# Second MLP's first product in pairs of tiles by Strassen's seven quarter products, in a fused attention and two-MLP kernel

## The chip, the core and the metric

The kernel runs on one core of a Trainium2 chip. The metric is the device time of one launch in microseconds (us). Engines are named TensorE (PE in the profile, its weight loads PEld), VectorE (DVE), ScalarE (ACT), GpSimd (POOL) and SyncE (SP, which issues all transfers here).

## What is computed

A linear attention with 4 batches, 8 heads, 576 positions and head size 64 gives 2304 rows of 512 values. Two MLPs follow, and it is the second that matters here:

```python
def _moe_ref(x, w_in, w_out):            # 2304 x 512, 512 x 2048, 2048 x 512
    h = x @ w_in
    g = np.maximum(0.01 * h, h)
    return (g @ w_out).astype(np.float32)

def _moe2_ref(x, w_in, w_out, g_ln):     # 2304 x 512, 512 x 1024, 1024 x 512
    h = x @ w_in
    h_max = np.max(h, axis=-1, keepdims=True)
    e = np.exp(h - h_max)
    sm = e / (np.sum(e, axis=-1, keepdims=True) + 1e-09)
    solu = h * sm
    mu = np.mean(solu, axis=-1, keepdims=True)
    var = np.mean((solu - mu) ** 2, axis=-1, keepdims=True)
    ln = (solu - mu) / np.sqrt(var + 1e-06) * g_ln
    return (ln @ w_out).astype(np.float32)
```

## The kernel before

**Tiles.** The 2304 rows are 18 tiles of 128, and for MLP 1 nine blocks j of two tiles. Large products run in float16 with each operand split into a high and a low half, and three of the four half products are taken: (high, high), (high, low), (low, high). So the first product of MLP 2 for one tile (`mlp2_in`) is 3 x 4 x 2 = 24 matmuls of 512 columns, into a PSUM tile `h2` of two banks, and the second product (`mlp2_out`) is 3 x 8 = 24 more into one bank of `h1`. MLP 1's first product is `st1` (tile `h1`, eight steps p for a block, L1090), its second `st2` (tile `y`, L1134).

**Order.** No engine's order is written out by hand. Every step is a generator that asks a planner (class `Issue`) for an engine with an expected duration and a priority; the planner runs a clock of its own, gives each free engine the waiting step with the lowest number, and emits instructions in that order. On the chip every engine then works through its queue in that order and waits by semaphores. `get` and `put` take and give back room (a PSUM bank, a buffer), `wait` and `set` are events. The numbers here: `st2` 1000, `st1` 1001.5, `mlp2_out` 1002, `mlp2_in` 1003 for tiles 0 to 12 and 1001 for the last five (`X["tail"]`). MLP 2 begins when its weights have been split ("mlp2").

**One tile of MLP 2 before.** After the 24 matmuls `mlp2_mid` takes the row maximum on VectorE (L1274), the exponential on ScalarE (L1279), the product with e (L1286, PSUM read again, after which `h2` is free), statistics (L1291), a power on GpSimd (L1294), the normalization (L1299), the high half on GpSimd (L1304) and the low half on VectorE (L1306), then two transposes through the DMA queue (L1311) into `lnT`, of which there are two. `mlp2_out` (L1324) multiplies, ScalarE copies the result out (L1333), SyncE stores it (L1339). Weights: `w1` and `w2` hold those of MLP 1, `W["i"]` (wi) and `W["o"]` (wo) those of MLP 2. `XY[j]` holds the transposed halves of block j's rows, first as input of MLP 1, later as input of MLP 2. `y_cut` makes the latter; `u` is the factor that undoes the scalings.

Of the kernel before, what the change touches and what calls it, by code (L numbers as in the profile page):

```python
# [23 lines left out]

X = {'NF': 1, 'bufs': {'qe': 3, 'v': 1, 'qf': 2, 'ke': 3, 'hl': 1, 'x': 2, 'g': 9, 'sg': 1, 'qT': 2, 'x16': 2, 'scr': 2, 'T': 1, 'wraw': 4, 'raw': 1, 'y16': 3, 'lnT': 2, 'l16': 2, 'kf': 4, 'v16': 3}, 't0': 38.107, 'tb': 187.479, 'w1': 54.105, 'w1s': -59.238, 'w2': 352.332, 'w2s': 14.253, 'b0': -113.048, 'b1': -6.038, 'dk': 42.281, 'dq': 74.634, 'dl': 206.254, 'c1': -41.937, 'c2': -59.523, 'pw2': 104.035, 'wlo': [1, 3, 8, 11, 13, 14, 16, 17, 25, 28, 31, 34, 36, 37, 38, 39], 'vd': 105.739, 'warm': 300, 'psq': ['k0', 'q0', 'q3', 'k6', 'q6', 'q7', 'q8', 'q9'], 'ep': ['k1', 'k12', 'k14', 'k16', 'k3', 'k4', 'k5', 'k6', 'k7', 'q0', 'q1'], 'te': ['k00', 'k01', 'k11', 'k40', 'k41', 'x10', 'x11'], 'KH': [2, 3], 'vb': 118.863, 'ya': [0, 1, 4, 6, 7, 9, 11, 12, 13, 14, 15, 16, 17, 18, 19, 20, 22, 23, 24, 27, 29, 31], 'EK': [0, 1, 2, 3, 6, 7, 8], 'pkv': 56.661, 'tail': 5, 'off': {'q1': -150.9, 'w15': 261.17, 'w4': 14.2, 'w23': -532.04, 'w18': 143.18, 'w24': -228.68, 'w28': 52.21, 'q10': 208.4, 'k8': -54.41, 'q5': 362.46, 'w7': 254.87, 'w25': 296.88, 'w12': 299.75, 'w9': -116.63, 'w19': 106.43, 'w31': 120.17, 'w27': -435.77, 'k11': -354.41, 'q16': -125.64, 'w5': 228.93, 'k9': -15.0, 'q2': 245.68, 'w8': 98.43, 'w14': -147.85, 'w30': -294.84, 'e1': 30.87, 'w26': 198.68, 'k13': 18.32, 'q0': 10.8, 'k0': -175.63, 'k7': 93.8, 'q13': 199.99, 'k2': -2.3, 'k16': -339.39, 'w22': -96.81, 'k6': -286.1, 'k4': 122.7, 'q8': 12.64, 'v0': -2.93, 'w20': -418.66, 'w16': 175.2, 'w0': 352.98, 'q6': 324.81, 'v2': 1.52, 'w17': -233.24, 'w13': 60.91, 'w3': -282.06, 'v1': 51.23, 'e2': 80.0, 'w1': 21.19, 'k15': -13.38, 'q3': -61.35, 'w2': -459.82, 'q7': 171.44, 'q4': 93.37, 'w11': 210.27, 'q12': -65.87, 'k5': 105.62, 'q15': 86.28, 'w10': 85.38, 'k14': -4.24, 'w29': -114.4, 'q17': -227.35, 'k12': -171.67, 'v3': 295.13, 'w21': -21.91, 'q11': -31.65, 'q9': 12.76, 'k17': 83.15, 'q14': 50.45, 'k1': 72.93, 'e3': 132.73, 'w6': -32.87, 'k3': -224.59, 'k10': 456.53}, 'pe': -535.604}

# [154 lines left out]
def linear_attention_moe_kernel(  # L181
# [92 lines left out]
    def t1(nm, n=1):  # L274
        return tiny.tile([128, n], F32, name=nm, tag=nm, bufs=12 if nm in ("sq", "sc", "s") else 8)

# [20 lines left out]
    def chain(c):  # L297
        return (True,) if c else ()
# [886 lines left out]
    def mlp2_weights():  # L1185
# [16 lines left out]
        stage.close()  # L1202
        P2["e"] = ctx.enter_context(tc.tile_pool(name="e2", bufs=2, side="right"))
        yield "set", "mlp2"

    def mlp2_weight(nm, src, sp, wp, gl):
# [15 lines left out]
        def fin(r):  # L1222
            yield from scale_of_max(r, inv, s)
            if nm == "i":
# [14 lines left out]
    def mlp2_in(a, z):  # L1239
        yield "wait", "mlp2"  # L1240
        for i in range(a, z):
# [4 lines left out]
            for j, (a, w) in enumerate(((0, 0), (0, 1), (KC, 0))):  # L1246
# [5 lines left out]
                yield "op", "PE", 1.71, mm, *chain(j < 2)  # L1252
            yield "go", mlp2_mid(i, ps.rearrange("p a f -> p (a f)")), i
        if z < NTILE:
            yield "go", mlp2_in(z, NTILE), 1001

# [12 lines left out]
    def mlp2_mid(i, ps):  # L1269
# [45 lines left out]
    def mlp2_out():  # L1315
        for i in range(NTILE):
# [51 lines left out]
    with tc.manual_schedule():  # L1368
# [57 lines left out]
```

## Time and profile before

| | |
|---|---|
| Median of 3 runs | 709.07 us (708.9 to 710.46) |
| Span of the profiled execution, first to last instruction | 707.2 us |
| TensorE busy / VectorE busy | 692.8 / 481.4 us |
| ScalarE busy / GpSimd busy | 361.5 / 132.8 us |
| Mean granted clock of TensorE | 0.998 of full speed |

How to read it: the profile is one execution; the runs are timed apart from it, over the whole launch, so the median stands somewhat above the span. [...] In the chain that ended last each step is followed back to what released it. In the last quarter of the span the kernel runs nothing but MLP 2.

### The profile page before, as it was taken

The numbers are of one execution on the slowest core, as the hardware profiler recorded it, in microseconds if no ns is written. First come the engines' busy times: TensorE is split into PE (matmuls) and PEld (weight loads), VectorE is DVE, ScalarE is ACT, GpSimd is POOL, SyncE is SP. The second block draws the span as 40 slices with busy tenths as digits, with TensorE's granted clock in tenths as the row PEclk, the third lists the DMA queues.
The fourth block names the chain that finished last, engine by engine and source line by source line (L and its number), as shares of the span: only waits on it lengthen the run. The fifth ranks groups of instructions, "written<-read, shape, count | busy, mean of one in ns | idle before, by whom it ended". The sixth has DMA issues, their size and how long they took to land.

```text
span 707.2 us, 13423 instructions
## 1 busy us (share of the span) xinstructions
PE 692.8 (98%) x5162; PEld 457.2 (65%) x5162; DVE 481.4 (68%) x1191; ACT 361.5 (51%) x770; POOL 132.8 (19%) x177
## 2 busy tenths in 40 slices
PE   7989999999999999999999999999999999999997
PEld 7889885587775667767676767676654444444443
DVE  6878888798765666756856478842267757757870
ACT  4768987797766664666745437463232122111211
POOL 2010220432311110011201022632001101101220
PEclk9999999999999999999999999999999999999999
DMA  9886986694735433722745667101013442432254
GB/s 289 239 255 195 251 237 142 123 180 112 148 72 94 96 71 84 120 67 52 130 76 89 126 216 192 66 1 30 1 31 75 104 75 54 102 69 60 59 103 106
DMA packets 183599, 81.22 MB, mean 115 GB/s; under 512 B 146416, under 2 KB 175088, under 8 KB 183536
## 3 DMA queue, kind: packets, MB, share of 16 engines
q1 hardware_dynamic: 183536, 80.37, 49.0%
q8 instruction: 40, 0.66, 0.4%
q14 instruction: 23, 0.19, 0.1%
HBM read 41.75 MB, written 4.72 MB: 66 GB/s over the span
## 4 chain that ended last, share of the span: by engine, by line
PE 75%; issue 7%; DMA 6%; ACT 5%; DVE 4%; POOL 1%; SPq 0%; POOLq 0%; ACTq 0%; DVEq 0%
PE h L1090 17%; PE y L1134 16%; PE h L1324 13%; PE h L1250 13%; DMA v<-in_v_dram 4%; PE h L1084 4%; PE kv L850 3%; ACT qe L786 2%; PE y L1130 1%; PE a L1008 1%; DVE mx L771 1%; PE a L763 1%; PE a L764 1%; DMA qT<-qf 1%; ACT ke L786 1%
## 5 line engine op out<-in xcount | busy, mean ns | idle before, releaser
L1134 PE MATMUL y<-w,g 128*128 128x512 f16 x768 | 176.0, 379 | 0.0
L1090 PEld LDWEIGHTS <-w 128*128 128x128 f16 x1536 | 148.2, 98 | 25.1 <-issue 1.1
L1134 PEld LDWEIGHTS <-g 128*128 128x128 f16 x768 | 73.9, 98 | 77.3 <-DVE g L1108 0.7
L1090 PE MATMUL h<-xy,w 128*128 128x256 f16 x960 | 111.8, 273 | 0.0
L1324 PE MATMUL h<-wo,lnT 128*128 128x512 f16 x432 | 96.0, 379 | 0.0
L1108 DVE TENSOR_TENSOR g<-h,g 128x512 f16<-128x512 f32 x64 | 44.0, 687 | 54.7 <-ACT g L1107 54.5
L1324 PEld LDWEIGHTS <-lnT 128*128 128x128 f16 x432 | 42.3, 98 | 51.0
L1250 PE MATMUL h<-wi,xy 128*128 128x512 f16 x336 | 75.1, 379 | 0.0
L1106 ACT ACTIVATE h<-h 128x512 f32<-128x512 f32 x64 | 38.1, 595 | 71.3 <-PE h L1090 70.9
L1090 PE MATMUL h<-xT,w 128*128 128x256 f16 x576 | 67.8, 273 | 0.1
L1279 ACT ACTIVATE e<-h,nb,u 128x1024 f32<-128x1024 f32 x18 | 21.7, 1203 | 76.5 <-DVE nb L1276 76.5
L1250 PEld LDWEIGHTS <-xy 128*128 128x128 f16 x336 | 32.9, 98 | 38.6
L786 ACT ACTIVATE qe<-a,nb,sc 128x128 f32<-128x128 f32 x128 | 47.1, 468 | 15.2 <-DVE nb L777 13.8
L771 DVE TENSOR_REDUCE mx<-a 128x4 f32<-128x512 f32 x63 | 41.4, 683 | 9.8 <-PE a L764 7.3
L1333 ACT ACTIVATE osb<-h,c_out 128x512 f32<-128x512 f32 x18 | 12.3, 686 | 64.4 <-PE h L1324 42.1
L873 POOL TENSOR_SCALAR qf<-qe 128x512 f16<-128x512 f32 x32 | 20.3, 634 | 110.4 <-ACT qe L786 84.5
L1107 ACT ACTIVATE g<-h 128x512 f16<-128x512 f32 x64 | 38.7, 604 | 1.2
L1294 POOL TENSOR_TENSOR rs<-ve,mhalf 128x1 f32<-128x1 f32 x18 | 9.9, 549 | 151.7 <-DVE ve L1293 151.7
L876 DVE SCALAR_TENSOR_TENSOR qf<-qe,qf 128x512 f16<-128x512 f32 x32 | 23.6, 738 | 16.0 <-POOL qf L873 16.0
L786 ACT ACTIVATE ke<-a,nb,sc 128x128 f32<-128x128 f32 x64 | 23.3, 468 | 16.8 <-DVE nb L777 15.0
L672 POOL TENSOR_TENSOR scr<-raw 128x1024 f32<-128x1024 f32 (+1 forms) x8 | 14.4, 1801 | 91.1 <-DMA raw<-in_q_dram 80.8
L1274 DVE TENSOR_REDUCE mx<-h 128x1 f32<-128x1024 f32 x18 | 21.9, 1216 | 12.1 <-PE h L1250 12.1
(197 smaller groups left out, 1146.0 us busy)
## 6 DMA issues: line engine op xcount, KB each, us to landing
wraw<-in_moe_w_in_dram SPq DMA_DIRECT2D x24, 512.0 KB, 5.7
wraw<-in_moe_w_out_dram SPq DMA_DIRECT2D x24, 512.0 KB, 4.7
v<-in_v_dram SPq DMA_DIRECT2D x12, 512.0 KB, 4.4
raw<-in_k_dram SPq DMA_DIRECT2D x8, 512.0 KB, 4.2
raw<-in_q_dram SPq DMA_DIRECT2D x8, 512.0 KB, 4.7
out_dram<-osb SPq DMA_DIRECT2D x16, 256.0 KB, 2.4
v<-in_v_dram SPq DMA_DIRECT2D x6, 128.0 KB, 3.7
lnT<-l SPq DMA_TRANSPOSE x36, 3.2
```

Source lines behind the costliest of these rows:

```text
L771: yield "op", "V", 0.6, lambda: V.tensor_reduce(out=u["mx"][:, hh::2], in_=w["ps"], axis=AX.X, op=ALU.max)
L786: A.activation(out=x[:, h, :], in_=w["ps"][:, h, :], func=AF.Exp, scale=st["sc"], bias=u["nb"][:, 2 * h + hh:2 * h + hh + 1])
L876: yield "op", "V" if stay else "V2", 0.62, lambda: V.scalar_tensor_tensor(out=w["f"][:, :, 1, :], in0=w["e"], scalar=2.0 ** 14, in1=w["f"] ...
L1084: PE.matmul(ps[:, f, :], lhsT=stash(w1, c * KC + kc)[:, o:o + 128], rhs=xT[j][:, kc, :], start=(kc == 0), stop=(kc == KC - 1))
L1090: PE.matmul(ps[:, f, :], lhsT=w1[:, c * KC + kc, w, o:o + 128], rhs=xT[j][:, :, xo + kc, :], start=(n == 0), stop=(n == 3 * KC - 1))
L1106: yield "op", "A", 0.48, lambda: A.activation(out=ps, in_=ps, func=AF.Prelu, scale=2.0 ** -19, alpha=0.01)
L1107: yield "op", "A", 0.48, lambda: A.activation(out=gg[:, 0], in_=ps, func=AF.Copy)
L1108: yield "op", "V", 0.6, lambda: V.tensor_tensor(out=gg[:, 1], in0=ps, in1=gg[:, 0], op=ALU.subtract)
L1134: PE.matmul(y_ps[j][t], lhsT=gg[:, a, f, ts], rhs=w2[:, 2 * p + f, w, :], start=(ends[0] and f == 0 and n == 0), stop=(ends[1] and f == 1 ...
L1250: PE.matmul(ps[:, f, :], lhsT=yT[i][:, a + c, :], rhs=W["i"][:, 2 * c + f, w, :], start=(j == 0 and c == 0), stop=(j == 2 and c == KC - 1))
L1274: yield "op", "V", 1.13, lambda: V.tensor_reduce(out=mx, in_=ps, axis=AX.X, op=ALU.max)
L1324: PE.matmul(ps, lhsT=t[:, a, f, :], rhs=W["o"][:, f, w, :], start=(j == 0 and f == 0), stop=(j == 2 and f == KF2 - 1))
```

## The change

Tiles 0 to 3 go as before. From tile 4 on two tiles j are taken together (`mlp2_pairs`). The pair's input is cut in quarters (tile, half of the 512 inputs), the weights in quarters (half of the inputs, half of the 1024 outputs), and the four result quarters come from seven quarter products instead of eight (Strassen's scheme in Winograd's form). One quarter product is 3 x 2 = 6 matmuls of 512 columns. Five of the seven take a sum of input quarters, of weight quarters, or both:

- `weight_sums` makes four sums of weight quarters (`T_`), for two input chunks c: high and low halves are added to float32, quarters subtracted, and the sums split in halves again (`sum_cut`). The first set adds on VectorE, the second on GpSimd (`X["wv"]`). They go into the place of `w1`, when `st1` of the last block has used it.
- `x_sums` makes four sums of input quarters (`S_`) for each pair, also in the place of `w1`; one float32 buffer (`S32`), three split ones (`S16`).
- In `mlp2_pairs` one PSUM half `pa` is written three times, each time on top of the former, and ScalarE copies it out after each (`seen`). VectorE adds such a copy to the other products and in the same instruction takes the row maximum (`joined`, a `tensor_tensor_reduce`). The results, `h`, lie in SBUF in six buffers (`H`): four in the place of `w2`, two in that of `XY[0]` and `XY[1]`.
- `pair_mid` and `pair_ln` do what `mlp2_mid` did: exponentials, the product with e fused with the sum for the mean, squares on ScalarE for the variance, scaling on ScalarE, halves, transposes. `lnT` gets four more buffers in the place of `w2`.
- Some scalings are one or two powers of two smaller. The table X loses `tail: 5` and gets `first: 2` (two blocks as before), `nh: 4`, `ws: 500`, `wv: [4, 0]`. Priorities: pairs 1001, their seventh product 1000.5, sums of weights 500, sums of inputs j - 1.

```diff
         if z < NTILE:
-            yield "go", mlp2_in(z, NTILE), 1001
+            yield "go", mlp2_pairs(z // 2, NB), 1001
...
+    def sums_open():
+
+        yield "wait", "w2i"
+        for c in range(2):
+            yield "go", weight_sums(c), X["ws"] + c
+        for p in range(6, 8):
+            yield "wait", ("s1", NB - 1, p)
+        yield "put", "S32"
...
+            for n in (8, 10, 14):
+                free_s.append(region(w1, n, 2).rearrange("p (a t k m) -> p a t k m", a=2, t=2, m=128))
+                yield "put", "S16"
...
+        for n in range(8):
+            yield "wait", ("s2", NB - 1, n)
+            if n < X["nh"]:
+                free_h.append(region(w2, 2 * n, 2).bitcast(F32))
+                yield "put", "H"
+            else:
+                free_t.append(region(w2, 2 * n, 2).rearrange("p (a f m) -> p a f m", a=2, m=128))
+                yield "put", "lnT"
...
+    def weight_sums(c):
+
+        b0, t0 = (0, 4) if c == 0 else (8, 0)
+        for p in range(4) if c == 0 else range(4, 6):
+            yield "wait", ("s1", NB - 1, p)
+        if c:
+            yield "wait", ("T", 0)
+        x = [region(w1, b0 + b, 1).bitcast(F32) for b in range(4)]
...
+        def whole(b, n):
+            if b < X["wv"][c]:
+                return "op", "V2", 0.69, lambda: V.tensor_tensor(out=x[b], in0=W["i"][:, n, 0], in1=W["i"][:, n, 1],
+                                                                op=ALU.add)
+            return "op", "G", 1.3, lambda: G.tensor_tensor(out=x[b], in0=W["i"][:, n, 0], in1=W["i"][:, n, 1],
+                                                           op=ALU.add)
...
+        for b in (0, 1):
+            yield "wait", ("B", c, b)
+        yield less(b11, b12, b11)
+        yield "go", sum_cut(c, 0, t0, b11), X["ws"] + c
...
+    def sum_cut(c, k, t0, t):
+        d = w1[:, t0 + k]
+        yield "op", "A", 0.61, lambda: A.activation(out=d[:, 0], in_=t, func=AF.Copy)
+        yield "op", "V2", 0.67, lambda: V.tensor_tensor(out=d[:, 1], in0=t, in1=d[:, 0], op=ALU.subtract)
+        yield "set", ("T", c, k)
+
+    def x_sums(j):
+
+        for t in range(2):
+            yield "wait", ("y", 2 * j + t)
+        yield "get", "S32"
+        y = XY[j]
+        r = region(w1, 12, 2).bitcast(F32).rearrange("p (t k m) -> p t k m", t=2, m=128)
+        yield "op", "V2", 1.24, lambda: V.tensor_tensor(out=r, in0=y[:, :, 0:KC], in1=y[:, :, KC:], op=ALU.add)
...
+        for o, a, b, op in ((a22, a21, a22, ALU.add), (a21, a11, a21, ALU.subtract), (a11, a22, a11, ALU.subtract),
+                            (a12, a12, a11, ALU.subtract)):
+            yield "op", "V2", 0.36, lambda o=o, a=a, b=b, op=op: V.tensor_tensor(out=o, in0=a, in1=b, op=op)
+        yield "get", "S16"
+        t = free_s.pop()
+        yield "op", "A", 1.2, lambda: A.activation(out=t[:, 0], in_=r, func=AF.Copy)
+        yield "op", "V2", 1.22, lambda: V.tensor_tensor(out=t[:, 1], in0=r, in1=t[:, 0], op=ALU.subtract)
+        yield "put", "S32"
...
+    def mlp2_pairs(a, z):
+
+        def product(dst, lhs, rhs, fresh):
+            def mm():
+                for n, (x, w) in enumerate(((0, 0), (0, 1), (1, 0))):
+                    for c in range(2):
+                        PE.matmul(dst, lhsT=lhs(x, c), rhs=rhs(w, c), start=(fresh and n == c == 0),
+                                  stop=(n == 2 and c == 1), skip_group_check=True)
+            return "op", "PE", 1.3, mm
...
+        for j in range(a, z):
+            yield "wait", ("S", j)
...
+            def A_(t, k):
+                return lambda x, c, y=y: y[:, t, x * KC + 2 * k + c, :]
+
+            def S_(t, k):
+                return lambda x, c, s=s: s[:, x, t, 2 * k + c, :]
...
+            def B_(k, f):
+                return lambda w, c: wi[:, 4 * k + 2 * c + f, w, :]
+
+            def T_(k):
+                return lambda w, c: w1[:, 4 - 4 * c + k - 1, w, :]
...
+            pa, pc = ps[:, 0], ps[:, 1]
+            yield "get", "y"
+            pb = mk(ps_y, "y", [128, DM], F32)
+            yield *product(pa, A_(0, 0), B_(0, 0), True), True
+            yield "go", seen(j, pa, h[0][:, 0:512], "p1"), j
+            yield *product(pb, A_(0, 1), B_(1, 0), True), True
+            yield "go", joined(j, pb, h[0][:, 0:512], u, 0, "p1", "c11"), j
+            yield *product(pc, S_(1, 1), T_(1), True), True
+            yield "wait", ("p1", j)
+            yield "get", "y"
+            pd = mk(ps_y, "y", [128, DM], F32)
+            yield *product(pa, S_(0, 0), T_(2), False), True
+            yield "go", seen(j, pa, h[0][:, 512:], "u2"), j
+            yield *product(pd, A_(1, 1), T_(4), True), True
+            yield "wait", ("u2", j)
+            yield product(pa, S_(1, 0), T_(3), False)
+            yield "go", seen(j, pa, h[1][:, 0:512], "u3"), j
+            yield "go", joined(j, pc, h[1][:, 512:], u, 2, "u3", "c22", h[1][:, 0:512]), j
+            yield "go", joined(j, pd, h[1][:, 0:512], u, 3, "c22", "c21"), j
+            yield "go", last_product(j, pc, h, u, product(pc, S_(0, 1), B_(1, 1), False)), 1000.5
+            yield "go", pair_mid(j, u), j
+
+    def last_product(j, pc, h, u, op):
+
+        yield "wait", ("c22", j)
+        yield op
+        yield "go", joined(j, pc, h[0][:, 512:], u, 1, "c11", "c12"), j
...
+    def seen(j, ps, o, name):
+
+        yield "op", "A", 0.6, lambda: A.activation(out=o, in_=ps, func=AF.Copy)
+        yield "set", (name, j)
...
+    def joined(j, ps, o, u, n, after, name, a=None):
+
+        yield "wait", (after, j)
...
+        else:
+            emit = lambda: V.tensor_tensor_reduce(out=o, in0=ps, in1=a, scale=1.0, scalar=init, op0=ALU.add,
+                                                  op1=ALU.max, accum_out=mx[:, n:n + 1])
+        yield "op", "V", 0.72, emit
+        if name in ("c11", "c21"):
+            yield "put", "y"
+        elif name == "c12":
+            yield "put", "h2"
+        yield "set", (name, j)
...
+    def pair_mid(j, st):
...
+        for t in range(2):
+            yield "get", "e2"
+            e[t] = mk(e2, "e2", [128, DF2], F32)
+            yield "op", "A", 1.2, lambda t=t: A.activation(out=e[t], in_=h[t], func=AF.Exp, scale=u[:, t:t + 1],
+                                                           bias=nb[:, t:t + 1], accum_out=sm[:, t:t + 1])
...
+        for t in range(2):
+            yield "op", "V2", 1.28, lambda t=t: V.tensor_tensor_reduce(
+                out=h[t], in0=h[t], in1=e[t], scale=r[:, t:t + 1], scalar=0.0, op0=ALU.mult, op1=ALU.add,
+                accum_out=tot[:, t:t + 1])
...
+        for t in range(2):
+            yield "op", "A", 1.2, lambda t=t: A.activation(out=e[t], in_=h[t], func=AF.Square, bias=nmu[:, t:t + 1],
+                                                           accum_out=vs[:, t:t + 1])
+            yield "put", "e2"
...
+        for t in range(2):
+            yield "go", pair_ln(2 * j + t, h[t], nmu[:, t:t + 1], rs[:, t:t + 1]), 2 * j + t
...
+    def pair_ln(i, h, nmu, rs):
+        yield "op", "A", 1.2, lambda: A.activation(out=h, in_=h, func=AF.Identity, scale=rs, bias=nmu)
...
+        yield "op", "G", 1.04, lambda: G.tensor_scalar(out=l16[:, 0], in0=h, scalar1=1.0, scalar2=1.0,
+                                                      op0=ALU.mult, op1=ALU.mult)
+        yield "op", "V2", 1.22, lambda: V.tensor_tensor(out=l16[:, 1], in0=h, in1=l16[:, 0], op=ALU.subtract)
+        free_h.append(h)
+        yield "put", "H"
...
-        sch.go(mlp2_in(0, NTILE - X["tail"]), 1003)
+        sch.go(mlp2_in(0, 2 * X["first"]), 1003)
+        sch.go(sums_open(), 500)
+        for j in range(X["first"], NB):
+            sch.go(x_sums(j), j - 1)
```

What this makes of the instruction order. TensorE at the start of the first pair (h_ tiles are PSUM, y the other PSUM pool; w_101 is `w1`'s place, with the sums; LDWEIGHTS rows left out). Before:

```order
L1250 MATMUL h_7348<-wi,xy_2993 128x512
...
L1324 MATMUL h_7393<-wo,lnT 128x512
...
L1250 MATMUL h_7403<-wi,xT 128x512
...
L1250 MATMUL h_7487<-wi,xT 128x512
...
L1324 MATMUL h_7518<-wo,lnT 128x512
```

After:

```order
L1255 MATMUL h_7351<-wi,xy_2993 128x512
...
L1373 MATMUL h_7445<-wi,xT 128x512
...
L1373 MATMUL y<-wi,xT 128x512
...
L1373 MATMUL h_7445<-w_101 128x512
...
L1373 MATMUL y<-w_101,xT 128x512
...
L1373 MATMUL h_7445<-w_101 128x512
...
L1578 MATMUL h_7491<-wo,lnT_6935 128x512
...
L1373 MATMUL h_7445<-wi,w_101 128x512
```

Each row stands for 6 matmuls (the first row with w_101 for 12, the output product for 16; in the list before for 24, the row with h_7487 for 16). The seventh product, the last row, has moved behind a part of an output product.

VectorE in the same stage. Before, one tile, from its maximum to its product with e:

```order
L1274 TENSOR_REDUCE mx_7777<-h_7693 128x1
L1265 TENSOR_SCALAR u<-ix_tok,iy_tok,c_h_98 128x1
L1276 TENSOR_SCALAR nb_7778<-mx_7777,u 128x1
L1283 TENSOR_SCALAR sm<-sm 128x1
L1284 RECIPROCAL r_7780<-sm 128x1
L1285 TENSOR_SCALAR r_7780<-r_7780,u 128x1
L1286 SCALAR_TENSOR_TENSOR so<-h_7693,r_7780,e_7808 128x1024
```

After, from the products with e of one pair (w_102 is `w2`'s place, with h) to the operation that the next pair's seventh product waits for; ISA is the fused form, and the ISA row behind it reads out the accumulator:

```order
L1482 ISA w_102,nmup<-w_102,e_7561,smp 128x1024
L1482 ISA nmup 128x1
L1354 TENSOR_TENSOR w_101<-xy_1954 128x1024
L1482 ISA w_102,nmup<-w_102,e_7582,smp 128x1024
...
L1358 TENSOR_TENSOR w_101<-w_101 128x256
L1485 TENSOR_SCALAR nmup<-nmup 128x2
L1456 SCALAR_TENSOR_TENSOR up<-ix_tok,c_h_98,iy_tok 128x2
L1358 TENSOR_TENSOR w_101<-w_101 128x256
L1444 ISA w_102,mxp<-h_7551,w_102 128x512
```

The operation that frees the PSUM half (last row) now stands behind another pair's products with e and a third pair's sums.

## Rows read from the trace of the kernel before

**Rows 1.** The page's head: span; busy us, share of span, instructions by engine.

```profile
span 707.2 us, 13423 instructions
...
PE 692.8 (98%) x5162; PEld 457.2 (65%) x5162; DVE 481.4 (68%) x1191; ACT 361.5 (51%) x770; POOL 132.8 (19%) x177
```

**Rows 2.** Three stretches: length, busy us by engine (count), clock, DMA share, GB/s.

```profile
487.00:525.00 38.00, 38.00 (x237) 23.04 (x236) 11.37 (x20) 7.19 (x12) 1.60 (x2) 1.00 0.08 15
525.00:542.00 17.00, 17.00 (x81) 7.72 (x79) 11.50 (x30) 5.70 (x11) 1.60 (x2) 1.00 0.37 78
542.00:645.00 103.00, 103.00 (x479) 46.69 (x478) 69.08 (x140) 19.82 (x30) 15.91 (x20) 1.00 0.36 77
```

**Rows 3.** Chain that ended last: start us, us, engine, tile, line, count.

```profile
531.73 10.36 PE h L1250 x48
542.09 5.18 PE h L1324 x24
...
673.32 29.37 PE h L1324 x136
```

**Rows 4.** Timeline of the end: start us, us, engine, line, operation.

```profile
699.70 2.97 PE L1324 MATMUL h<-wo,lnT 128*128 128x512 f16 x13
...
703.47 1.13 SPq L1342 DMA_DIRECT2D out_dram<-osb  x2
```

**Rows 5.** Groups by line and shape, VectorE, ScalarE, GpSimd: busy us, mean ns.

```profile
L1108 DVE TENSOR_TENSOR g<-h,g 128x512 f16<-128x512 f32 x64 | 44.0, 687 | 54.7 <-ACT g L1107 54.5
...
L1286 DVE SCALAR_TENSOR_TENSOR so<-h,r,e 128x1024 f32<-128x1024 f32 x18 | 23.1, 1284 | 0.6
...
L1306 DVE TENSOR_TENSOR l<-e,l 128x1024 f16<-128x1024 f32 x18 | 22.0, 1220 | 8.8 <-POOL l L1304 8.8
...
L1022 DVE TENSOR_TENSOR a<-a,rd 128x256 f32<-128x256 f32 x32 | 13.6, 429 | 0.5
...
L876 DVE SCALAR_TENSOR_TENSOR kf<-ke,kf 128x512 f16<-128x512 f32 x12 | 8.3, 688 | 9.0 <-POOL kf L873 9.0
...
L1293 DVE TENSOR_SCALAR ve<-mv 128x1 f32<-128x1 f32 x18 | 2.7, 150 | 0.4
...
L1107 ACT ACTIVATE g<-h 128x512 f16<-128x512 f32 x64 | 38.7, 604 | 1.2
...
L1279 ACT ACTIVATE e<-h,nb,u 128x1024 f32<-128x1024 f32 x18 | 21.7, 1203 | 76.5 <-DVE nb L1276 76.5
...
L692 ACT ACTIVATE hl<-raw,s 128x1024 f16<-128x1024 f32 x12 | 14.3, 1190 | 0.0
...
L1333 ACT ACTIVATE osb<-h,c_out 128x512 f32<-128x512 f32 x18 | 12.3, 686 | 64.4 <-PE h L1324 42.1 <-issue 22.3
...
L1279 ACT ACTIVATION_READ_ACCUMULATOR e<-h,nb,u 128x1 f32 x18 | 3.4, 191 | 0.0
...
L337 POOL TENSOR_TENSOR wo<-wo 128x512 f16<-128x512 f32 x5 | 5.8, 1154 | 0.4
```

**Rows 6.** Timeline of VectorE, 485 to 508 us; idle us before each in brackets.

```profile
494.04 0.69 DVE L1108 TENSOR_TENSOR g<-h,g 128x512 f16<-128x512 f32 x1 [9.58 <-ACT g L1107]
500.97 0.69 DVE L1108 TENSOR_TENSOR g<-h,g 128x512 f16<-128x512 f32 x1 [6.24 <-ACT g L1107]
507.91 0.69 DVE L1108 TENSOR_TENSOR g<-h,g 128x512 f16<-128x512 f32 x1 [6.25 <-ACT g L1107]
```

**Rows 7.** Timeline of TensorE about 525 and 542 us.

```profile
525.09 1.89 PE L1324 MATMUL h<-wo,lnT 128*128 128x512 f16 x8
...
541.92 5.34 PE L1324 MATMUL h<-wo,lnT 128*128 128x512 f16 x24
```

**Rows 8.** Timeline of VectorE, two rows in succession at 542 us.

```profile
541.87 0.69 DVE L1291 BATCH_NORM_STATS2 bn<-so 128x6 f32<-128x512 f32 x1
542.48 1.21 DVE L1274 TENSOR_REDUCE mx<-h 128x1 f32<-128x1024 f32 x1
```

**Rows 9.** DMA issues on the page: KB or count, median us to landing.

```profile
lnT<-l SPq DMA_TRANSPOSE x36, 3.2
```

More of the change, by code (lines that the diff above doesn't have):

```diff
@@ L268, in linear_attention_moe_kernel @@
     BUFS.update(X["bufs"])
-    sch = Issue(dict(BUFS, g0=NG0, g=NG, pair=1, two=1, v16=0))
+    sch = Issue(dict(BUFS, g0=NG0, g=NG, pair=1, two=1, v16=0, S16=0, S32=0, H=0))
     def mk(pool, tag, shape, dt):
@@ L274, in t1, with t2 @@
     def t1(nm, n=1):
-        return tiny.tile([128, n], F32, name=nm, tag=nm, bufs=12 if nm in ("sq", "sc", "s") else 8)
+        return tiny.tile([128, n], F32, name=nm, tag=nm, bufs=12 if nm in ("sq", "sc", "s") else 4 if nm in ("mv", "ve") else 8)
+    def t2(nm, n=2):
+        return tiny.tile([128, n], F32, name=nm, tag=nm, bufs=3)
     ident = const.tile([128, 128], F32, name="ident")
@@ L1203, in mlp2_weights @@
         P2["e"] = ctx.enter_context(tc.tile_pool(name="e2", bufs=2, side="right"))
+        for n in range(BUFS["lnT"]):
+            free_t.append(P2["e"].tile([128, 2, KF2, 128], F16, name=f"lnT{n}", bufs=1))
         yield "set", "mlp2"
@@ L1222, in fin @@
         def fin(r):
-            yield from scale_of_max(r, inv, s)
+            yield from scale_of_max(r, inv, s, 12 if nm == "i" else 14)
             if nm == "i":
@@ L1253, in mlp2_in, with region @@
             yield "go", mlp2_mid(i, ps.rearrange("p a f -> p (a f)")), i
+            yield "set", ("in", i)
         if z < NTILE:
-            yield "go", mlp2_in(z, NTILE), 1001
+            yield "go", mlp2_pairs(z // 2, NB), 1001
+    def region(w, n, k):
+        return w[:, n:n + k].rearrange("p n a f -> p (n a f)")
+    S16, free_h, free_s, free_t = {}, [], [], []
+    def sums_open():
[6 more added lines that the diff above has]
+        for c in range(2):
+            yield "wait", ("T", c)
+            if c == 0:
+                continue
+            for n in (8, 10, 14):
+                free_s.append(region(w1, n, 2).rearrange("p (a t k m) -> p a t k m", a=2, t=2, m=128))
+                yield "put", "S16"
+        for j in range(2):
+            yield "go", more_h(j), 0
+        for n in range(8):
[6 more added lines that the diff above has]
+                yield "put", "lnT"
@@ new lines, in more_h, with less, one @@
+    def more_h(j):
+        yield "wait", ("in", 2 * j + 1)
+        free_h.append(XY[j].rearrange("p t k m -> p (t k m)").bitcast(F32))
+        yield "put", "H"
[12 more added lines that the diff above has]
+                                                           op=ALU.add)
+        def less(o, a, b):
+            return "op", "V2", 0.69, lambda: V.tensor_tensor(out=o, in0=a, in1=b, op=ALU.subtract)
+        def one(b, n):
+            yield whole(b, n)
+            yield "set", ("B", c, b)
+        for b, n in enumerate((2 * c, 2 * c + 1, 2 * c + 4, 2 * c + 5)):
+            yield "go", one(b, n), X["ws"] + c
+        b11, b12, b21, b22 = x
+        for b in (0, 1):
+            yield "wait", ("B", c, b)
+        yield less(b11, b12, b11)
+        yield "go", sum_cut(c, 0, t0, b11), X["ws"] + c
+        yield "wait", ("B", c, 3)
+        yield less(b12, b22, b12)
+        yield "go", sum_cut(c, 2, t0, b12), X["ws"] + c
+        yield less(b22, b22, b11)
+        yield "go", sum_cut(c, 1, t0, b22), X["ws"] + c
+        yield "wait", ("B", c, 2)
+        yield less(b21, b22, b21)
+        yield "go", sum_cut(c, 3, t0, b21), X["ws"] + c
+        for k in range(4):
+            yield "wait", ("T", c, k)
+        yield "set", ("T", c)
@@ new lines, in sum_cut @@
+    def sum_cut(c, k, t0, t):
[10 more added lines that the diff above has]
+        yield "op", "V2", 1.24, lambda: V.tensor_tensor(out=r, in0=y[:, :, 0:KC], in1=y[:, :, KC:], op=ALU.add)
+        (a11, a12), (a21, a22) = ((r[:, t, 0:2], r[:, t, 2:4]) for t in range(2))
+        for o, a, b, op in ((a22, a21, a22, ALU.add), (a21, a11, a21, ALU.subtract), (a11, a22, a11, ALU.subtract),
[6 more added lines that the diff above has]
+        yield "put", "S32"
+        S16[j] = t
+        yield "set", ("S", j)
@@ L1326, in mlp2_out @@
                 yield "op", "PE", 1.71, mm, *chain(j < 2)
+            free_t.append(t)
             yield "put", "lnT"
```

59 lines of the change are left out of this document (54 added, 5 removed).

## The prediction

> **What bounds the kernel now.** I read the page's head first, then stretches of the second half, then the chain that ended last, then the single instructions. The head shows TensorE busy 692.8 us of a span of 707.2 us [rows 1]. Busy time alone proves little, so I look at the stage that is changed. [...] The chain of the last 175 us is TensorE at nearly every step: 24 matmuls of 512 columns take 5.18 us on it, 48 take 10.36 [rows 3]. That is 0.216 us for one, with nothing between them. So in this stage a matmul less is 0.216 us less, as long as nothing else becomes late. Behind the last matmul stand one ScalarE copy and the last store, and the span ends 4.5 us after the matmuls do [rows 4]; the change leaves that tail alone.
>
> **What the change removes.** Two tiles of the first product of MLP 2 take 2 x 24 = 48 matmuls; a pair takes seven products of 6, so 42. Seven pairs (tiles 4 to 17) save 7 x 6 = 42 matmuls of the same form, 42 x 0.216 = 9.07 us. The program agrees: TensorE has 84 rows less, 42 matmuls and 42 weight loads. Its order is the same as before, row for row, until the last but one step of the second product of MLP 1 has been issued, at 525.09 us [rows 7]. The profiled span of 707.2 us would become 698.1; the median of the runs is 709.07, 1.9 us above that span, and I carry that over: **700.0 us if TensorE never waits**. All that follows asks how much it waits.
>
> **What it adds on VectorE, per pair.** The x sums: two operations of 1024 elements at 1.22 (nearest row L1306) and four of 256 at 0.43 (nearest L1022), 4.2 us. Four fused operations that finish a quarter and take its maximum: 512 elements from PSUM and SBUF took 0.69 (L1108); each is followed by a readout of one element per partition, of which this trace has only cousins, 0.15 on VectorE (L1293) and 0.19 on ScalarE (L1279's readout). I take 0.84 with the readout, since L1293 is VectorE's own; ends 0.69 and 0.88; 3.4 us for four. Two fused products with e: 1.28 (L1286) and a readout, 2.9 us. Two low halves at 1.22 (L1306), 2.4 us. Eight small ones of 0.15 to 0.25, 1.5 us. Sum 14.4 us [rows 5]. Before, 69.08 us of VectorE stood beside 479 matmuls, that is ten tiles of 48 [rows 2]: 6.9 us a tile, 13.8 for two. So VectorE has about as much to do as before. But its work now lies closer together: from the first pair's first product to the last one's seventh the new order has 478 matmuls, 103 us, for all seven pairs, 14.7 us each.
>
> **ScalarE, per pair.** Three copies of a half at 0.60 (L1107), one copy of the x sums at 1.19 (L692), two exponentials and two squares at 1.20 with a readout of 0.19 (L1279), two scalings at 1.19, two output copies at 0.69 (L1333): 12.3 us, against 4.2 before [rows 5]. In 14.7 us this fits. GpSimd has less than before.
>
> **The quarter sums of the weights** come once: 8 sums, four of them on GpSimd at 1.15 (L337), 8 differences and 8 low halves; 20 operations of 0.69 on VectorE, 13.8 us, and 8 ScalarE copies. They lie between 484 and 521 us, where VectorE sat idle for 9.58, 6.24 and 6.25 us [rows 6]. What covers them is this idle time; without it they would cost up to 13.8 us. Behind them on VectorE queue the last cuts of g (L1108), and behind those TensorE's second product; the first ten must be through by 500.97 us, and from 494.7 us, after the cut before, there are 6.2 us for eight of them at 0.69, less an overlap of some 0.07 each: 5.0 us. Cost 0.
>
> **Start of the first pair.** From 525.09 us the new order has 8 + 6 + 16 + 24 + 24 = 78 matmuls before the first pair, 16.8 us, so it starts at 541.9, where the old order had its second output product [rows 7]. By then VectorE must have done the sums of two pairs and what tiles 0 to 2 need. Its rows from 521.8 us to the first fused operation add up to some 20 us: done at 541 to 542.5, wanted at 544.5, after 12 matmuls of the pair. Cost 0, cover 2 us.
>
> **Inside a pair** one PSUM half is written three times, with a ScalarE copy out between. The first copy has 12 matmuls (2.6 us) of cover for its 0.60 us; the second only 6 (1.3 us) in five of the pairs and 14 in two. A copy that finds a 1.2 us operation just begun ahead of it is up to 0.5 us late there. The seventh product waits for a fused operation that stands behind everything else in VectorE's queue. I walk that queue with the durations above. First pair: from 544.7 us 12 operations, 8.2 us, less overlap: done at 552.2, and the seventh product comes 52 matmuls after 541.9, at 553.1. From there to the next pair's: 16.2 us of VectorE against 15.5 of TensorE and 0.9 in hand; then 13.6 against 14.7; then 15.9 against 16.0. These sums of durations are too long, since an operation starts some 0.07 us ahead of the end of the one before (L1291 at 541.87 for 0.69, the next at 542.48 [rows 8]), 1.5 us in 22 of them; so VectorE stays 1 to 2 us ahead at each. The last two pairs have no x sums beside them and have more. At the end 224 matmuls of output products, 48 us, stand behind the last seventh product; the chain from there to the last transposed tile (two exponentials, products, squares, scalings, low halves at some 1.2 to 1.4 each, and transposes that land after 3.2 [rows 9]) is some 20 us, so the end has no hole. The balance is close, so I add 1.2 us of waits: **701.2 us**.
>
> [...] L876 works on two SBUF operands, f32 and f16, and took 688 ns for 512 elements [rows 5], as long as L1108 with one operand in PSUM. [...]
>
> **Rivals.**
> (a) The fused products with e, a new instruction on two f32 SBUF operands, run at half rate: 1.28 becomes some 2.4 (twice L1286 less one fixed part), 2.2 us more per pair against 1 to 2 us in hand: six pairs lose 0.3 to 1.2 us each, 2 to 7 us, 702 to 707, say 704. For: no row of this operation. Against: L876 and L1286. Chance 0.06. [...]
> (b) ScalarE is late: its queue is three times as full, and a copy behind an exponential that itself waits for VectorE holds TensorE's third write. Seven pairs x 0.3 to 0.8 us: 702.5 to 706, say 704. Chance 0.15.
> (c) All fused operations, those from PSUM too, run at half rate: 4 x 0.53 + 2 x 1.1 = 4.3 us more per pair, less 1.5 in hand, 2.8 x 7 = 20 us of waits: 720, **slower**. It decides from about 0.45 us more per operation: 6 x 0.45 = 2.7, less 1.5, x 7 = 8.4 us, which eats the gain. For: none of them runs in this trace. Against: L1108, L876 and L1286, three forms of two operands at the same rate. Chance 0.08.
> (d) The matmuls go but not the time: the sums end late, g or the first pair waits for them 6 to 9 us, 706 to 709.5. For: GpSimd's four sums stand ahead of the second set. Against: the gaps of [rows 6]. Chance 0.05.
>
> **How the numbers follow.** Forecast 701.2 with waits of 0 to 2.5 us, 700 to 702.5: chance 0.66. With (a) and (b), up to 706, it is 0.87, and I end the range there; below it reaches 699.4, since there are no fewer matmuls and only the spread of runs is left. A measurement of this kernel can tell 0.2% (1.4 us) from no change. Faster by more than that is below 707.6: the forecast, (a), (b) and a small part of (d), 0.88; within, 0.04; slower, (c), 0.08.
>
> **What would show it.** In the profile after: TensorE busy throughout from 487 us to its end, which comes 9 us earlier; no wait of a seventh product or a third write longer than 1 us; fused operations of 0.69 and 1.28 us with readouts of 0.15; L1108's rows up to 508 us at their old times; the first pair at 542 us. Wrong would be: a fused row of over 1.1 us (512 elements) or 2 us (1024); third writes that wait for ScalarE; a first pair after 545 us.

## The result, and the profile after

The prediction was 701.2 us. The runs give a median of **701.69 us** (701.04 to 706.56), beside 709.77 us for the kernel before on the same chip; the ratio is 0.9888, 95% interval 0.9851 to 0.9925. The span of the profiled execution fell from 707.2 to 700.0 us.

The three stretches of [rows 2], after (length, busy us by engine with counts, clock, DMA share, GB/s):

```profile
487.00:525.00 38.00, 38.00 (x238) 23.01 (x236) 22.54 (x40) 12.01 (x20) 7.37 (x6) 1.00 0.01 3
525.00:542.00 17.00, 17.00 (x80) 7.72 (x79) 15.37 (x38) 7.59 (x13) 1.94 (x2) 1.00 0.36 75
542.00:645.00 103.00, 102.25 (x474) 46.27 (x473) 83.61 (x182) 60.12 (x89) 20.43 (x19) 1.00 0.40 79
```

TensorE is as full as before, at the same granted clock of 1.00, and short of full by 0.75 us of 103. VectorE went from 69 to 84 us, ScalarE from 20 to 60. One wait of TensorE is left in the whole second half:

```profile
PE h L1373 <- ACT w L1431: 0.7, 1, 0.7
```

Its place, in pair 5, TensorE and then ScalarE (start us, us, engine, line; in brackets the idle time before, and what ended it):

```profile
587.35 1.46 PE L1373 MATMUL h<-wi,xy 128*128 128x512 f16 x6
...
589.94 1.46 PE L1373 MATMUL h<-w 128*128 128x512 f16 x6
592.15 1.46 PE L1373 MATMUL h<-w 128*128 128x512 f16 x6 [0.74 <-ACT w L1431]
```

```profile
589.51 0.19 ACT L1476 ACTIVATION_READ_ACCUMULATOR e<-xy,nbp,up 128x1 f32 x1
591.50 0.60 ACT L1431 ACTIVATE w<-h 128x512 f32<-128x512 f32 x1 [1.80 <-PE h L1373]
```

From 589.94 to 592.15 are 2.21 us where six matmuls take 6 x 0.216 = 1.30: this wait costs 0.91 us, 0.17 more than the idle time shown, since the row of six is itself 1.46 us long.

**A clean measure.** VectorE's first cut of g after 490 us stood at 494.04 [rows 6] and stands at 495.01 after, although nothing ahead of it on TensorE was changed. In the twelve runs below it moves from 492.5 to 497.7, although TensorE's order is the same up to 525 us in all of them; TensorE's waits in the first half come out differently from run to run (those for transfers add up to 5.0 us before and 4.3 after). So I measure from that row to the end of the span: **213.2 us before, 205.0 after**. The sum is 213.16 - 42 x 0.216 + 0.91 = 205.0. For every kernel I also add up what TensorE loses from 490 us on (distances of successive rows less 0.216 us per matmul of 512 columns):

| Kernel | Matmuls against before | Lost by TensorE, us | Row of g to end, us | Ratio to before (95%) |
|---|---|---|---|---|
| before | 0 | 0 | 213.2 | 1 |
| changed; a second time | -42 | 0.91; 0.91 | 205.0; 205.0 | 0.9888; 0.9876 (0.9858 to 0.9895) |
| eight products | 0 | 0.91 | 214.1 | 1.0008 (0.9989 to 1.0026) |
| no pairs | 0 | 10.4 | 223.6 | 1.0129 (1.0096 to 1.0162) |
| no pairs, old tail rule | 0 | 0 | 213.2 | 0.9990 (0.9968 to 1.0011) |
| maximum apart | -42 | 3.9 | 208.0 | 0.9919 (0.9891 to 0.9947) |
| low halves twice | -42 | 4.0 | 208.1 | 0.9946 (0.9926 to 0.9967) |
| low halves three times | -42 | 19.8 | 223.9 | 1.0147 (1.0103 to 1.0191) |
| early copy | -42 | 0.6 | 204.7 | 0.9871 (0.9846 to 0.9896) |
| eight pairs | -48 | 4.7 | 207.5 | 0.9926 (0.9902 to 0.9951) |
| high half on ScalarE | -42 | 0.91 | 205.0 | 0.9861 (0.9843 to 0.9878) |
| eight pairs, early copy and high half on ScalarE | -48 | 5.3 | 208.1 | 0.9918 (0.9897 to 0.9938) |
| seven pairs, early copy and high half on ScalarE | -42 | 2.9 | 207.0 | 0.9888 (0.9864 to 0.9912) |

In every row the stretch is 213.16, less 0.216 for each matmul fewer, plus what TensorE lost, to 0.1 us; behind TensorE's last matmul every one of these kernels ends after 4.5 us. So TensorE alone sets the length of the stretch, with its matmuls, its waits and, in two of the kernels, slower matmuls behind a long wait (below).

### The profile page after: what moved, and what is told of

The parts are those of the page before. It is cut to its first block, busy times and chain, and to the rows that moved or that the text cites. A ratio compares the mean times of both kernels' runs of the same rounds, so it can differ in the third digit from the quotient of the medians.

```text
span 700.0 us, 13443 instructions
## 1 busy us (share of the span) xinstructions
PE 684.4 (98%) x5120; PEld 453.4 (65%) x5120; DVE 486.6 (70%) x1211; ACT 416.1 (59%) x848; POOL 139.9 (20%) x174
## 4 chain that ended last, share of the span: by engine, by line
PE 74%; issue 7%; DMA 6%; ACT 6%; DVE 4%; POOL 1%; SPq 1%; POOLq 0%; ACTq 0%; DVEq 0%
PE h L1093 18%; PE y L1137 16%; PE h L1578 13%; PE h L1373 6%; PE h L1087 3%; PE h L1255 3%; PE y L1373 3%; PE kv L853 2%; ACT qe L789 2%; PE y L1133 2%; DMA v<-in_v_dram 2%; PE a L1011 1%; DVE mx L774 1%; DMA raw<-in_k_dram 1%; DMA scr<-in_omega_dram 1%
## 5 line engine op out<-in xcount | busy, mean ns | idle before, releaser
L1093 PEld LDWEIGHTS <-w 128*128 128x128 f16 x1536 | 148.2, 98 | 25.1 <-issue 1.1
L1111 DVE TENSOR_TENSOR g<-h,g 128x512 f16<-128x512 f32 x64 | 44.0, 688 | 45.6 <-ACT g L1110 45.4
L1578 PE MATMUL h<-wo,w 128*128 128x512 f16 x288 | 64.1, 379 | 0.0
L1578 PEld LDWEIGHTS <-w 128*128 128x128 f16 x288 | 28.2, 98 | 34.0
L1588 ACT ACTIVATE osb<-h,c_out 128x512 f32<-128x512 f32 x18 | 12.3, 682 | 44.0 <-PE h L1578 41.1
L675 POOL TENSOR_TENSOR scr<-raw 128x1024 f32<-128x1024 f32 (+1 forms) x8 | 14.4, 1805 | 91.3 <-DMA raw<-in_q_dram 81.1
L1578 PE MATMUL h<-wo,lnT 128*128 128x512 f16 x144 | 32.2, 379 | 0.0
L1373 PE MATMUL h<-w 128*128 128x512 f16 x126 | 29.8, 379 | 0.7 <-ACT w L1431 0.7
L667 DVE TENSOR_REDUCE sq<-scr 128x16 f32<-128x1024 f32 (+1 forms) x20 | 22.1, 1107 | 11.5 <-POOL scr L675 7.6
L1373 PEld LDWEIGHTS <-w 128*128 128x128 f16 x168 | 16.4, 98 | 20.7 <-issue 1.0
L1087 PE MATMUL h<-xT,w 128*128 128x256 f32 x128 | 29.7, 383 | 0.0
```

The lines of the kernel that those rows point to most:

```text
L667: yield "op", "V", 0.07 + 0.54 * m, lambda: V.tensor_reduce(out=st["sq"], in_=tiles(st["scr"]), axis=AX.X, op=ALU.add)
L1087: PE.matmul(ps[:, f, :], lhsT=stash(w1, c * KC + kc)[:, o:o + 128], rhs=xT[j][:, kc, :], start=(kc == 0), stop=(kc == KC - 1))
L1093: PE.matmul(ps[:, f, :], lhsT=w1[:, c * KC + kc, w, o:o + 128], rhs=xT[j][:, :, xo + kc, :], start=(n == 0), stop=(n == 3 * KC - 1))
L1111: yield "op", "V", 0.6, lambda: V.tensor_tensor(out=gg[:, 1], in0=ps, in1=gg[:, 0], op=ALU.subtract)
L1373: PE.matmul(dst, lhsT=lhs(x, c), rhs=rhs(w, c), start=(fresh and n == c == 0), stop=(n == 2 and c == 1), skip_group_check=True)
```

## Experiments

**Is it the matmuls?** The fifth product of each pair is made twice.

```diff
-            yield *product(pd, A_(1, 1), T_(4), True), True
+            yield *product(pd, A_(1, 1), T_(4), True, 2), True
```

> Each pair makes its fifth product twice, so TensorE has eight products of 6 matmuls again, in the order of the changed kernel; everything else is as in the changed kernel. Theory (the gain is TensorE's 42 matmuls and nothing else): 42 x 0.216 = 9.07 us come back, less at most the one wait of 0.74 us that the longer products may hide: span 708.3 to 709.1, time 710 to 711, level with the kernel before. Rival (the gain comes from the other parts, such as the buffers, the fused operations or the order, and TensorE was not the bound): span stays at 700 to 703.

214.1 us, 9.1 more than the changed kernel, with the same wait of 0.74: the whole gain is gone and the ratio to before is 1.0008. The matmuls, with their weight loads, carry it all.

**Do the weight sums cost anything?** First all tiles in the old way, with the sums kept, then with the old rule for the last five tiles as well.

```diff
-'first': 2
+'first': 9
```

> All tiles take the old 24 matmuls; the quarter sums of the weights are still made, and not used; the lower transposed buffers stay as in the changed kernel. Theory (the weight sums lie in VectorE's idle time between 485 and 521 us and cost nothing): the time of the kernel before, 708.9 to 710.5. Rival (the sums cost 1 to 5 us by delaying g or the first product of MLP 2, hidden so far in the gain of the pairs): 711 to 715.

Neither: 719.13 us. From 490 us on TensorE does not wait until 690, and then twice (TensorE, the last rows):

```profile
693.26 5.35 PE L1578 MATMUL h<-wo,w 128*128 128x512 f16 x24 [2.47 <-DMA w<-l]
703.91 7.67 PE L1578 MATMUL h<-wo,w 128*128 128x512 f16 x24 [5.29 <-DMA w<-l]
```

The last tiles' first products now stand at the end, and their transposes come late. After the wait of 5.29 us the last 24 matmuls took 7.67 us in place of 5.35. I had overlooked that the change also takes out the old tail rule.

```diff
-        sch.go(mlp2_in(0, 2 * X["first"]), 1003)
+        sch.go(mlp2_in(0, NTILE - X["tail"]), 1003)
```

> No pairs, the weight sums still made, and the last five tiles' first products moved ahead of their place again, by the rule of the kernel before that the change took out. Theory (the 7.8 us of waits in the run without pairs are that rule's, since they stand at the last two output products, and the weight sums cost nothing): TensorE without a wait from 487 us to its end, span 706 to 708.5, time 708 to 711. Rival (the waits come from the moved buffers or the sums): 5 us or more of waits stay at the end, span over 712.

213.2 us, as before, and TensorE full from 487 us to the end of its work. So the sums are free, though VectorE and ScalarE do them:

```profile
487.00:525.00 38.00, 38.00 (x237) 23.07 (x236) 22.75 (x42) 12.95 (x23) 6.46 (x6) 1.00 0.08 15
```

**How near is VectorE?** The maximum apart, then the low halves two and three times.

```diff
-            emit = lambda: V.tensor_tensor_reduce(out=o, in0=ps, in1=a, ..., op0=ALU.add, op1=ALU.max, ...)
+            V.tensor_tensor(out=o, in0=ps, in1=a, op=ALU.add)
+            if n % 2:
+                V.tensor_reduce(out=mx[:, n:n + 1], in_=u["h"][n // 2], axis=AX.X, op=ALU.max)
...
+        for _ in range(2):  # or 3
             V.tensor_tensor(out=l16[:, 1], in0=h, in1=l16[:, 0], op=ALU.subtract)
```

> The maximum is taken apart: each fused operation becomes a plain addition or subtraction, and two reductions of 1024 elements (1.21 us each by the old kernel's reduction) per pair follow, in the same places of VectorE's order; four readouts of 0.08 us go. That is 2.1 us more on VectorE for each pair. Theory (VectorE is 1 to 2 us ahead of TensorE at each seventh product): 0.1 to 1.1 us of waits in each of six pairs, 1 to 6 us, span 701 to 706. Rival (all of VectorE's idle time in this stage, 18.6 us of 102, 2.7 us a pair, can be used): no change, span 700.0. A third (the reductions stand ahead of the operations that end the seventh product's bank, so the whole 2.1 us shows in every pair): 14 us, span 714.

> The low half of each normalized tile of the pairs is computed twice by VectorE: 2 x 1.22 = 2.44 us more per pair, at the end of a tile's chain, in the unchanged order; the second time changes nothing. It is 0.3 us less than the 2.7 us per pair at which the prediction's rival (c) would have eaten the whole gain. Theory A (the prediction's walk: VectorE has 1 to 2 us in hand at each seventh product): 0.4 to 1.4 us of waits in each of six pairs, 3 to 8 us, span 703 to 708. Theory B (after the run with the maximum apart, which cost 1.9 us of span for 2.1 us per pair on the path of a pair itself: nearly all of VectorE's idle time, 2.7 us a pair, can be used): span 700 to 702.

> The same low half three times: 4.88 us more per pair on VectorE. Theory A (1 to 2 us in hand): 2.9 to 3.9 us of waits in each of six pairs, 17 to 23 us, span 717 to 723. Theory B (2.7 us in hand): 2.2 us in each of six pairs, 13 us, span 713, slower than the kernel before. Both have TensorE wait behind a fused operation or a copy in every pair; if the span stays under 707, VectorE was never near the limit and the balance of the prediction was wrong.

For 2.1 us a pair TensorE loses 3.0 us more than in the changed kernel, for 2.44 us 3.1, for 4.88 us 18.9. Counted from the changed kernel's row of g, the span would be 703.0 with the maximum apart, as the first theory has it (701 to 706); its rival (700.0) and the third theory (714) fall. With 2.44 us it would be 703.1: theory A (703 to 708) holds at its lower end, B (700 to 702) falls. With 4.88 us it would be 718.9, in A's range again.

But only the size came as in these theories, not the place. They went by VectorE's lead at the seventh products. With the maximum apart no seventh product waited for VectorE, and all three waits of over 0.1 us are for copies. With 2.44 us the seventh products lost 1.1 of the 4.0 us, with 4.88 us 1.9 of the 19.8. The longest waits are for copies by a ScalarE that itself waits for VectorE. Here is the longest (low halves three times, TensorE, then ScalarE):

```profile
626.42 1.46 PE L1373 MATMUL y<-wi,xy 128*128 128x512 f16 x6
631.74 5.28 PE L1373 MATMUL h<-w 128*128 128x512 f16 x12 [3.86 <-ACT xy L1431]
```

```profile
628.74 1.24 ACT L1498 ACTIVATE w<-w,nmup,rsp 128x1024 f32<-128x1024 f32 x1 [4.41 <-DVE nmup L1493]
...
631.11 0.57 ACT L1431 ACTIVATE xy<-h 128x512 f32<-128x512 f32 x1
```

ScalarE stood idle for 4.41 us, until VectorE had the bias of a scaling (L1498). Behind the scaling and an exponential stood the first copy of pair 7, and the third product, which writes the other half of the copied tile, waited for that copy. So a VectorE that falls behind reaches TensorE first through ScalarE's order. This is the mechanism of the prediction's rival (b), and not that of its walk along VectorE's queue.

The step from 2.44 to 4.88 is steep for two reasons: the waits add up once the room is used, and the longest wait cost twice, as the stretch from 631 to 637 us of the same run shows (columns as above):

```profile
631.00:637.00 6.00, 5.26 (x13) 1.87 (x13) 5.18 (x7) 3.04 (x6) 1.64 (x2) 0.50 0.29 55
```

After 3.86 us without a matmul the granted clock was 0.50 in this stretch, and 12 matmuls took 5.28 us in place of 2.75. In the same run a wait of 2.30 us was followed, six matmuls later, by six in 2.75 in place of 1.46 (granted clock 0.93 from 586 to 612 us); with the low halves twice, 12 matmuls behind a wait of 1.35 us kept to 2.75. Of the 19.8 us lost, some 6 are of this kind (1.7 at 593 us, 2.5 at 632, 1.7 behind a wait of 3.05 us at 685), the rest waits.

**The one wait.** Does ScalarE come late, or is it the order of issue?

```diff
-            yield *product(pc, S_(1, 1), T_(1), True), True
+            yield *product(pc, S_(1, 1), T_(1), True, copy), True   # issues the first copy, if not yet issued
```

> The first copy of each pair is issued at the latest just ahead of the third product, so that its wait for TensorE names the first product and not the third, which writes the other half of the same tile. Theory (the one wait of 0.74 us at 592 us, in pair 5, is this order of issue, and not a late ScalarE): the copy of pair 5 starts at about 589.7 in place of 591.5, the wait of the second write is gone, span 699.3, 0.7 us or 0.1% less. Rival (ScalarE is busy with the exponentials ahead of it): the wait stays, span 700.0.

The copy of pair 5 starts at 590.16, straight behind an exponential's readout, and no longer waits for the third product; in the changed kernel it began at 591.50 with ScalarE idle for 1.80 us, at the very end of that product (589.94 + 1.46). So the order of issue was the cause. But the gain is 0.3 us, less than half of what was expected: TensorE now loses 0.32 and 0.29 us at two third products, which wait for the copy ahead of them. The halves `pa` and `pc` are one tile, and a wait between them arises in either order. Two separate tiles might part them; that was not tried.

**Eight pairs.**

```diff
-'first': 2
+'first': 1
...
         yield op
+        yield "set", ("in", 2 * j + 1)
```

> Pairs from tile 2 on, eight pairs in place of seven: 6 matmuls, 1.3 us, less. In its order the first pair has 44 matmuls ahead of it after 526 us in place of 78, so it is wanted at 535.6 and its sums come from a VectorE that was through with its earlier work at about 541 to 542 in the changed kernel. Theory (VectorE's sums set the start of the first pair): TensorE waits 3 to 7 us before or inside the first two pairs, span 702 to 706. Rival (the start has no such bound): 1.3 us less, span 698.7.

207.5 us, 2.5 more than with seven. Three losses lie at the start, 0.78, 1.16 and 0.99 us:

```profile
531.87 1.45 PE L1373 MATMUL y<-wi,xy 128*128 128x512 f16 x6 [0.62 <-DVE y L331]
538.21 1.46 PE L1373 MATMUL h<-w 128*128 128x512 f16 x6 [1.00 <-ACT w L1432]
543.51 1.46 PE L1373 MATMUL h<-wi,w 128*128 128x512 f16 x6 [0.82 <-DVE mxp L1445]
```

The first wait is for VectorE's cut of MLP 1's last output (L331), which still reads a PSUM tile `y` such as the second product writes, and not for a sum: the first pair began at 529.79, and no product waited for its sums. The second is a third write that waits for the second copy, the third a seventh product that waits for VectorE. So the early start costs 2.9 us against the 1.3 that it saves, by a VectorE and a ScalarE that are not through with the tiles ahead, and not by late sums, as I had it. Two more losses follow at 568 and 573 us, 1.04 us at a seventh product and 0.70 at a copy; the one wait of the changed kernel is gone.

**VectorE beside GpSimd.** Five VectorE rows of the pairs took 1.74 to 2.06 us. Does GpSimd's high half stretch them?

```diff
-        yield "op", "G", 1.04, lambda: G.tensor_scalar(out=l16[:, 0], in0=h, ...)
+        yield "op", "A", 1.05, lambda: A.activation(out=l16[:, 0], in_=h, func=AF.Copy)
```

> The high half of the pairs' normalized tiles is made by ScalarE (a copy of 1.05 us) in place of GpSimd. Theory (five VectorE rows of 1024 elements took 1.74 to 2.06 us in the changed kernel, in place of 1.22 or 1.28, because a GpSimd operation on a tile ran beside them): no VectorE row of the pairs' 1024-element operations over 1.4 us, their means at 1.28 (products with e) and 1.22 (low halves), VectorE 3 us less busy from 542 to 645 us (80.5 in place of 83.6). TensorE has at most 0.7 us of waits more or less, since ScalarE has 60 of 103 us and gets 15 more: span within 1 us of the changed kernel, from the same start. Rival (the long rows are the operations' own): rows of 1.7 us and over stay.

It does: with the high half on ScalarE the longest such row took 1.29 us. Groups by line of VectorE (busy us, mean ns; ten of the fourteen tiles), the changed kernel and then this one:

```profile
L1482 DVE CUSTOM_DVE_ANT_0 w<-w,e,smp 128x1024 f32<-128x1024 f32 x10 | 14.3, 1434 | 0.1
L1503 DVE TENSOR_TENSOR l<-w,l 128x1024 f16<-128x1024 f32 x10 | 13.0, 1302 | 5.4 <-POOL l L1501 5.4
```

```profile
L1482 DVE CUSTOM_DVE_ANT_0 w<-w,e,smp 128x1024 f32<-128x1024 f32 x10 | 12.8, 1281 | 0.1
L1502 DVE TENSOR_TENSOR l<-w,l 128x1024 f16<-128x1024 f32 x10 | 12.1, 1222 | 4.0 <-ACT l L1501 3.8
```

VectorE worked 80.51 us from 542 to 645, as expected, in place of 83.61, and the stretch is 205.0 us again: at this load VectorE is not the bound.

**Together.** Both edits, the early copy and the high half on ScalarE, with eight and with seven pairs; and the changed kernel once more.

> Eight pairs, from tile 2 on, with the early first copy and the high half on ScalarE. Theory (in the run with eight pairs TensorE waited 3.8 us for VectorE and for copies, of which the three waits before 545 us, 2.4 us, come from the first pair's early start and stay, and the others come from a VectorE that is too slow): 2 to 3 us of waits, less 1.3 us of matmuls, so 0.5 to 1.5 us more than the changed kernel with its 0.74 us of waits from the same start. Better than the changed kernel (699.5 or less) only if the waits fall under 1.5 us.

> Seven pairs, with the early first copy and the high half on ScalarE. Theory (in the run with the high half on ScalarE the one wait of 0.69 us, at 635 us, is again a first copy issued behind the third product): no wait of TensorE over 0.2 us from 487 us to its end, and 0.6 to 0.7 us less from the same start than the changed kernel: span from VectorE's first cut of g after 490 us to the end 204.3 in place of 205.0. Rival (the copy was late because ScalarE is fuller): a wait of 0.3 to 1.3 us stays.

> The changed kernel itself, beside the run before it on the same chip. Theory: 0.6 to 0.7 us, 0.1%, slower than the kernel with both edits, less than the medians can tell apart; the stretch from VectorE's first cut of g after 490 us to the end is 205.0 again, with the one wait of 0.74 us, however early or late that stretch starts.

Neither mixture gains, and the theories of both missed. With eight pairs the stretch is 3.1 us longer than the changed kernel's, where 0.5 to 1.5 were expected: TensorE loses 5.3 us, 2.9 of them at the start, in the same three places, and 2.4 at products that wait for first copies. With seven pairs it loses 2.9 in four such places. The largest, 1.48, is a third product that waits for the early copy; the copy stands behind an exponential and a scaling, and ScalarE had been idle for 2.77 us ahead of that scaling, until VectorE had its bias. So it is less a fuller ScalarE, as the rival had it, than one that waits for VectorE. The changed kernel beside it had a stretch of 205.0 us again, with its one wait; it is not slower than the kernel with both edits but 2.0 us faster. So none of these kernels is measurably faster than the changed one; the best stretch, 204.7 us with the early copy alone, is 0.3 us better.

## Why the prediction was right, point by point

- **42 matmuls x 0.216 = 9.07 us on a saturated TensorE**: right. Eight products bring back 9.1.
- **1.2 us of waits**: 0.91 came, but at another place, so that the size agrees is luck. I feared the second copies (6 matmuls of cover) and the seventh products; none of these waited. The one wait was a first copy, which I had given 12 matmuls of cover: I took its release for the first product, and in pair 5 it was the third. The same happened in pair 3 (copy at 561.22, the end of the third product), where eight output matmuls covered it.
- **VectorE, 14.4 us a pair, 1 to 2 us in hand**: near. VectorE's rows of the pairs add up to 14.7 us a pair. Some terms were too large: readouts took 0.08 us, not 0.15, though the fused operations themselves 0.69 to 0.75 (the longer where the start value is an earlier maximum). Some rows were longer, by GpSimd, by 3.1 us in all. In the changed kernel each seventh product started 0.7 to 2.9 us after the readout that it needs, 1.9 in the middle. What the walk left out is the other way by which VectorE holds TensorE up: through ScalarE, which waits for VectorE and comes late with a copy. With more work on VectorE, that came first.
- **ScalarE, 12.3 us a pair**: right, its rows add up to 12.1 us a pair, and ScalarE is busy for 60 of 103 us. Rival (b) did not come in the changed kernel; it comes when VectorE has some 2 us more a pair, and when ScalarE also gets the high halves and the copy is early.
- **Weight sums free**: right, L1111 (L1108 before) keeps its 6.93 us steps and TensorE its rows; shown without pairs. **First pair at 541.9**: it began at 542.89, 0.97 later like all from the row of g on. **Tail**: no wait behind the last seventh product (645.67).
- **Rivals (a) and (c), half rate**: L1482 has two float32 operands in SBUF and took 1281 ns for 1024 elements with the high half on ScalarE, as L1286 did (1284) with one in PSUM [rows 5]; the fused operations of 512 elements took 0.69 to 0.75 us. Half rate was my supposition for instructions of which I had no row; no run shows it. My price for (c) seems too high: I had 2.7 us more a pair cost 8.4 us; 2.44 us cost 3.1 and 4.88 cost 18.9, so the gain is eaten somewhere between them. These runs had the extra work in the low halves, not in the fused operations. The loss there comes from waits that add up and then from matmuls at a lower clock (0.50 from 631 to 637 us with the low halves three times).
- **The agreement of the median is partly luck**: the start of the changed stretch moves by some microseconds from run to run; the stretch itself is what the sum predicted (213.16 - 9.07 + 1.2 = 205.3), to 0.3 us.

## What to carry to other kernels

Where one engine is full, price a change by that engine's instructions, and then walk every other engine's queue for what may make it wait, the waits between those engines included: here a late VectorE showed first as a late ScalarE. Measure from a row that both kernels share. A buffer of two halves that are written and read apart may do better as two tiles, since here a wait between the halves followed from the order of issue alone; no run shows what two tiles give. The product with e took 1.28 us beside GpSimd's high half with one operand in PSUM, and up to 2.06 us with both in SBUF: when an operand moves, count both engines.

## What the hardware showed that I had not expected

- **VectorE and GpSimd held each other up.** The changed kernel, 594 to 599 us:

```profile
594.53 1.13 POOL L1501 TENSOR_SCALAR l<-w 128x1024 f16<-128x1024 f32 x1 [6.01 <-ACT w L1498]
594.68 2.06 DVE L1482 CUSTOM_DVE_ANT_0 xy<-xy,e,smp 128x1024 f32<-128x1024 f32 x1
...
596.20 1.44 POOL L1501 TENSOR_SCALAR l<-w 128x1024 f16<-128x1024 f32 x1 [0.54 <-ACT w L1498]
...
596.66 2.04 DVE L1503 TENSOR_TENSOR l<-w,l 128x1024 f16<-128x1024 f32 x1
```

  In each of these overlaps the row that began second took longer: 1.28 became 2.06, then GpSimd's 1.04 became 1.44, then 1.22 became 2.04. It grew by 0.78, 0.40 and 0.82 us where 0.98, 0.54 and 0.98 us of the first were left. Had the first product run only behind GpSimd's row, it would have ended at 594.53 + 1.13 + 1.28 = 596.94; it ended at 596.74. Before, the product with e read one operand from PSUM, and its 15 rows from 542 us on had a mean of 1284 ns. Five of them ran beside GpSimd's high half, and neither grew longer:

```profile
546.55 1.04 POOL L1304 TENSOR_SCALAR l<-e 128x1024 f16<-128x1024 f32 x1 [1.19 <-DVE sm L1283]
...
546.94 1.28 DVE L1286 SCALAR_TENSOR_TENSOR so<-h,r,e 128x1024 f32<-128x1024 f32 x1
```

- **A fused operation's readout is short on VectorE**: means of 80 to 82 ns, beside 186 to 190 for those of the pairs' exponentials and squares on ScalarE.
- **TensorE's waits cost more than their idle time**: that of 0.74 us in the changed kernel 0.91, that of 1.35 with the low halves twice 1.51. Behind one of 3.86 us (low halves three times) the granted clock was 0.50 from 631 to 637 us.
